# Gated loop and feed-forward block on one core: two queues for the first gate load, and a later place for three weight fetches

## The chip, the cores and the metric

The kernel runs on one core of a Trainium2 chip. A core has a matrix engine (TensorE, PE in the profile; its weight loads are PEld), a vector engine (VectorE, DVE), a scalar engine (ScalarE, ACT), a general engine (GpSimd, POOL) and a queue engine (SyncE, SP). Transfers between the device memory and the core's own memory are issued by SP, ACT or POOL and carried by 16 DMA engines. Each engine works through its own list of instructions in order. The metric is the time of one execution on the device, in microseconds (us); the median of 7 runs of the kernel before is 748.93 us, from 748.06 to 753.47.

## The reference, cut to what matters

The input has 4 batches, 8 heads, 768 time steps and 48 features. A complex gate `a` first gets its magnitude limited, then drives a recurrence over time; its output goes through a feed-forward block of width 2048.

```python
mag = np.sqrt(a_re * a_re + a_im * a_im)
scale = np.minimum(mag, 0.999) / (mag + 1e-06)
a_re_n, a_im_n = (a_re * scale, a_im * scale)
for t in range(S):
    new_re = ar * S_re - ai * S_im
    new_im = ar * S_im + ai * S_re
    S_re, S_im = (new_re + k_t v_t^T, new_im)
    y[:, :, t] = q_t . S_re
x = y.transpose(0, 2, 1, 3).reshape(B * S, H * D)     # 3072 x 384
h = x @ w_in                                          # 384 x 2048
out = np.maximum(h, 0.0) ** 2 @ w_out                 # 2048 x 384
```

## The kernel before, in words

**Units.** The work is cut into 8 units: 4 batches, each in two halves of 384 time steps. A unit's 8 heads make 4 pairs, and two pairs make a half z of the unit (z = 0 and 1). For each unit the kernel

- loads `a`, `q`, `k` (per half z, real and imaginary part of `a` apart) and `v` (in three chunks);
- normalises `a` in elementwise steps on ACT and DVE: `sq` and `sqi` square the two parts, `m2` adds them, `ln`, `ex` and `s2` make an inverse root, `r1` and `r2` are a Newton step, `n1`, `n2`, `l1`, `l2` scale `a`;
- multiplies the gates up over time (`in..`, `tot`, a tree of `scan` products, `bk`, `xn`), which gives the decay up to each step;
- multiplies `q` and `k` by these decays (`f`, `P`, `QK`). The result is called Q~ and K~ below; in the code it is the tile `QK`;
- writes K~ to device memory in time order (`rows`) and reads it back in another layout (`KC`), pair by pair for units 0 and 1;
- per pair: transposes (`tq`), scores (`sa`), masks (`A`), multiplies K~ and v (`kv`), adds up the state (`S`), mixes (`mix`), copies out (`y`) and places the result in `xT` by DMA;
- runs the feed-forward block: 16 blocks `h` (three matmuls each; for the first three blocks the first two matmuls are a step of their own, `h0`), `relu` and `g` on ACT, and the projection `o` in 3 chunks of 4 parts.

**Weights.** They arrive as 64-bit numbers and are turned into 32-bit ones on the chip: 16 pieces of `w_in` and 16 of `w_out`, each with a fetch (384 KB), a step `lower` on ACT and three steps `cv` on DVE. The first 13 pieces wait only for the first unit's `a` (`gate`, a small POOL copy that really reads `a`). Pieces 13 to 15 reuse the buffers of pieces 0 to 2. The `w_in` pieces are fetched by POOL, the `w_out` pieces by SP.

**What sets the order.** Every step is entered with an engine, a cost, a delay until its result can be used (`lag`), a rank and a list of steps that it depends on. `lay_out` (line 579) goes through the steps like a scheduler and gives each a start in its own model of time; the instructions are then emitted in that order, and `emit` ties each engine's instructions to that order. The dependencies in these lists are the planner's: in the program, an instruction waits only where it shares data with another (a tile that it reads, or a buffer that it reuses). `queue` is SP for units 0 and 1 and POOL after them (line 762). `fetch` is line 648, `weight_steps` line 694, the loads are `load` and `load_v` (lines 772 and 780), `square` is line 816, and `rows` (line 1186) holds both the write (line 1194) and the read back (line 1201).

**The profile's lines.** L777 is every load of `a`, `q` and `k`, L783 that of `v`, L667 a weight fetch, L825 and L828 the squares of the first unit, L832 the sum, L835 the ACT steps after it, L840 the Newton steps, L1194 and L1201 the rows of K~ and the reading back (KC), L1320 `kv`, L1360 the copy before `xT`, L1367 the DMA into `xT`, L1437 `h`, L1454 `o`. L1094 is a matmul without use of its result (`busy`, ten steps of two instructions in each of the units 0 and 1).

Of the kernel before, what the change touches and what calls it, by code (L numbers as in the profile page):

```python
# [481 lines left out]
def fast_path(ctx, tc, q, k, v, a_re, a_im, moe_w_in, moe_w_out, out, flag):  # L482
# [211 lines left out]
    def weight_steps():  # L694
        for i in range(2 * NF):
            if i < FIRST:
                deps = [("gate", z) for z in range(2)]
            elif i < NF:
                deps = [("cv", i - FIRST, 2)]
            elif i in LENT:  # L700
                deps = [("mix", 0, NP - 1), ("xT", 0, NP - 1, 1)]
            elif i < NF + NRAW:
                deps = [("cv", i - (NF - NF // 2), 2)]
            else:
                deps = [("cv", i - NRAW - (len(LENT) if i < NF + 2 * NRAW + len(LENT) else 0),
                         2)]
            step(("fetch", i), "SP" if i >= NF else "POOL", 600 if i >= NF else 750, 400 + i,
                 deps, lambda i=i: fetch(i), 7000)
            rank = CONV[i // NF] + i
            step(("lower", i), "ACT", 470, rank, [("fetch", i), ("e2", 0, 1)], lambda i=i: lower(i))  # L710
            for part, cost in enumerate((270, 470, 470)):
                step(("cv", i, part), "DVE", cost, CONV[i // NF] + i // 2 * 6 + part * 2 + i % 2,
                     [("cv", i, part - 1), ("lower", i) if part == 2 else ("fetch", i),
                      ("ap", 0, 1)],
                     lambda i=i, part=part: convert(i, part))
# [42 lines left out]
    def chain_steps(u):  # L758
# [10 lines left out]
        def src(ap):  # L769
            return ap[u["b"], :, ts(u["half"], L), :]  # L770

        def load(name, z, j):
            if j == 0:
                u[name, z] = nat.tile([C, 2, HH, W, D], F32, name=f"{name}{z}",
                                      tag=f"{name}{z}")
            ap = {"a": (a_re, a_im), "qk": (q, k)}[name][j]
            get.dma_start(out=u[name, z][:, j].rearrange("p h c d -> p h (c d)"),  # L777
                          in_=src(ap)[ts(z, HH)].rearrange(LOADS, c=W))

        def load_v(j):  # L780
            if j == 0:
# [4 lines left out]
        for name in ("a", "qk"):  # L786
            for z in range(2):
                for j in range(2):
                    add(("ld", n, name, z, j), queue, issue,
                        [("f", n - 1, z, i, r) + x for i in range(2) for r in range(2)  # L790
                         for x in ((), (0,), (1,))]
                        if name == "a" else [("ap", n - 1, z)]
                        + [("KC", n - 1, 1, i) for i in (NP // 2, NP - 1)]
                        + ([("xT", 0, NP - 1, h) for h in range(2)] if n == 1 else []),
                        lambda name=name, z=z, j=j: load(name, z, j),
                        lag=(3100 + 1100 * z + 300 * j if name == "a" else 8000)
                        if n == 0 else 6000)
        for j in range(W):
            add(("v", n, j), queue, issue,
                [("mix", n - 2, NP - 1), ("kv", n - 2, NP - 1), ("rest", n - 2, 2)]  # L800
                + ([("e2", 0, 1)] if n == 1 else []),
                lambda j=j: load_v(j), lag=27000 if n == 0 else 8000)
        if n == 0:

# [10 lines left out]

        def square(z, r=None):

            if not r:
                u["fa", z] = wk.tile([C, 2, HH, W, D], F32, name=f"fa{z}", tag=f"fa{z}")
                u["fb", z] = wk.tile([C, 2, HH, W, D], F32, name=f"fb{z}", tag=f"fb{z}")  # L820
            if r is None:
                act.activation(out=whole(u["fa", z]), in_=whole(u["a", z]), func=AF.Square,
                               accum_out=sums[:, n, z:z + 1])
            elif r == 0:
                act.activation(out=parts(z)[0], in_=flat(u["a", z][:, 0]), func=AF.Square)  # L825
            else:
                a = flat(u["a", z][:, 1])
                dve.tensor_tensor(out=parts(z)[1], in0=a, in1=a, op=ALU.mult)  # L828
# [71 lines left out]

        D1, A1 = dve_cost(NEL), act_cost(NEL)
        if n == 0:
            one("sq", "ACT", A1, lambda z: [("ld", n, "a", z, 0)], lambda z: square(z, 0))
            one("sqi", "DVE", D1, lambda z: [("ld", n, "a", z, 1), ("sq",)],
                lambda z: square(z, 1))
            one("ms", "ACT", A1 + 90, lambda z: [("m2",), ("me",)],
                lambda z: measure(z, parts(z)[2], AF.Copy), rank=900)
            add(("minus",), "ACT", 190, [("me", 0, 1)],
                lambda: act.mul(out=minus, in_=ident, mul=-1.0), rank=910)
        else:  # L910
            one("sq", "ACT", act_cost(2 * NEL) + 90,
                lambda z: [("ld", n, "a", z, 1), ("ap", n - 1, z), ("carry", n - 1, 0)],
                square)
# [295 lines left out]
        for z in range(2):  # L1209
            of_z = range(z * NP // 2, (z + 1) * NP // 2)  # L1210
            was_read = [("tq", n - 1, i, c) for i in of_z for c in range(W)] + [
                ("rows", n - 1, z, i) for i in of_z]
            add(("ov", n, z), "DVE", D1, [("xn", n, 2), ("rest", n, z), ("kk", n, z)],
                lambda z=z: over_k(z), rank=late(z))
            done = []
            for i, r in ((i, r) for i in range(2) for r in range(2)):
                for j in range(2):
                    if early or i == 0:
                        add(("f", n, z, j, j ^ r) + ((i,) if early else ()), "DVE",
                            dve_cost(NEL // 2 if early else NEL),  # L1220
                            [("xn", n, j)] + scans[-1],
                            lambda z=z, j=j, r=r, i=i if early else None:
                            cross(z, j, j ^ r, i))
                if not early:
                    continue
                P = ("P", n, z, r, i)
                qk = [("QK", n, z, j, r, i) for j in (1, 0)]
                add(P, "PE", 970, [("f", n, z, 0, r, i), ("f", n, z, 1, 1 - r, i), ("ov", n, z)]
                    + was_read + [("minus",)], lambda z=z, r=r, i=i: join_pe(z, r, i),
                    rank=-3000 if z == 0 else -1950 + 40 * n, bank="sc", until=qk[1])  # L1230
                for j, key in zip((1, 0), qk):
                    add(key, "DVE", 410, [P, qk[0] if j == 0 else P],
                        lambda z=z, j=j, r=r, i=i: apply(z, j, r, i))
                    done.append(key)
            for r in () if early else range(2):
                add(("join", n, z, r), "DVE", D1, [("f", n, z, 0, r), ("f", n, z, 1, 1 - r)],
                    lambda z=z, r=r: join(z, r))
            if not early:
                for j in (1, 0):
                    for r in range(2):  # L1240
                        add(("QK", n, z, j, r), "DVE", D1,
                            [("join", n, z, r), ("ov", n, z)] + was_read,
                            lambda z=z, j=j, r=r: apply(z, j, r))
                        done.append(("QK", n, z, j, r))
            add(("ap", n, z), "DVE", 0, done, lambda: None)
            for i in pairs_of(z):
                whole_z = not early
                keys = [x for x in done if x[3] == 1 and (whole_z or x[5] == i % 2)]
                pairs = of_z if whole_z else [i]
                for name, lag, deps in (  # L1250
                        ("rows", 4800 if whole_z else 3800,
                         keys + [("KC", n - 1, z, x) for x in of_z]),
                        ("KC", 7000 if whole_z else 4200,
                         [("rows", n, z, pairs[0])] + [("kv", n - 1, x) for x in of_z])):
                    add((name, n, z, pairs[0]), "POOL", 750, deps,
                        lambda z=z, i=pairs[0], name=name: rows(z, i, name == "KC"),
                        rank=-100, lag=lag)
                    for x in pairs[1:]:
                        add((name, n, z, x), "POOL", 0, [(name, n, z, pairs[0])],
                            lambda: None)  # L1260
# [331 lines left out]
```

## Time and profile before

| what | value |
|---|---|
| median of 7 runs | 748.93 us (748.06 to 753.47) |
| the profiled execution, its own time | 749.56 us |
| its span from the first to the last instruction | 747.8 us |
| mean granted TensorE clock | 0.997 |
| PE busy | 706.0 us, 94% |
| DVE busy | 509.0 us, 68% |
| ACT busy | 411.9 us, 55% |
| POOL busy | 115.0 us, 15% |
| read from and written to device memory | 56.62 MB, 14.16 MB |

The page gives busy time by engine, the span in 40 slices, the DMA queues, the chain of work that ended last and the costliest groups. The answers of the trace give instructions in order of time with the idle time before each in brackets and what ended it, the waits of an engine added up, busy times by stretch, and for each DMA the time from its issue to its landing. An issue in such a list is the time in which a queue (SPq, ACTq, POOL) hands a transfer over, not the transfer. Idle time of an engine matters only where it is the one that the others wait for.

### The profile page before, as it was taken

How to read it: one execution, taken by the hardware profiler on the slowest of the kernel's cores; microseconds unless marked ns; L12 is line 12 of the kernel's file. 1: busy time of each engine (PE TensorE's matmuls, PEld its weight loads, DVE VectorE, ACT ScalarE, POOL GpSimd, SP SyncE). 2: the span in 40 equal slices, each digit the busy share in tenths (PEclk: the TensorE clock that was granted, in tenths of full speed). 3: DMA queues.
4: the chain of work that ended last, by engine and by line, in shares of the span. 5: the costliest groups of instructions: out<-in, count | busy, mean ns of one | idle time of the engine just before them, and what ended most of it. 6: DMA issues, size and time to landing. Idle time of an engine off the chain costs nothing.

```text
span 747.8 us, 10017 instructions
## 1 busy us (share of the span) xinstructions
PE 706.0 (94%) x3578; PEld 474.7 (63%) x3578; DVE 509.0 (68%) x1204; ACT 411.9 (55%) x764; POOL 115.0 (15%) x165
## 2 busy tenths in 40 slices
PE   0389999999999999999999999999999999999996
PEld 0258556586667767766775677677667655555553
DVE  5999999978698898799469896988971564000000
ACT  6556594266938658853976479677365204402500
POOL 5013100052013013012210211130020431000000
PEclk9999999999999999999999999999999999999999
DMA  9617750054026115224510431261032684000000
GB/s 265 199 59 210 260 189 12 21 168 129 1 74 198 29 50 168 82 59 128 163 46 3 161 120 29 63 200 49 27 109 82 193 292 170 0 24 11 1 11 25
DMA packets 39196, 76.25 MB, mean 102 GB/s; under 512 B 10881, under 2 KB 25313, under 8 KB 39137
## 3 DMA queue, kind: packets, MB, share of 16 engines
q0 software_dynamic: 14336, 53.88, 23.0%
q1 hardware_dynamic: 24672, 21.49, 9.4%
q8 instruction: 30, 0.49, 0.3%
q14 instruction: 30, 0.24, 0.1%
q10 hardware_dynamic: 128, 0.15, 0.1%
HBM read 56.62 MB, written 14.16 MB: 95 GB/s over the span
## 4 chain that ended last, share of the span: by engine, by line
PE 90%; DMA 3%; SPq 2%; DVE 2%; ACT 0%; issue 0%; ACTq 0%
PE o L1454 33%; PE h L1437 32%; PE sa L1306 6%; PE tq L1293 5%; PE kv L1320 3%; PE P L1177 2%; PE ypair L1345 2%; SPq L783 2%; DMA v<-in_v_dram 1%; PE ypair L1350 1%; PE bk L979 1%; DMA xT<-yt 1%; PE tot L979 1%; PE y L1345 1%; PE busy L1094 1%; SPq L777 1%
## 5 line engine op out<-in xcount | busy, mean ns | idle before, releaser
L1437 PE MATMUL h<-xT,w 128*128 128x384 f32 x768 | 257.0, 487 | 1.6 <-DMA xT<-yt 1.6
L1454 PE MATMUL o<-w,g 128*128 128x384 f32 x768 | 255.7, 487 | 0.0
L1454 PEld LDWEIGHTS o<-w,g 128*128 128x128 f32 x768 | 142.9, 190 | 91.8 <-issue 0.4
L1437 PEld LDWEIGHTS h<-xT,w 128*128 128x128 f32 x768 | 142.2, 190 | 92.7 <-issue 2.8
L1444 ACT ACTIVATE g<-h 128x384 f32<-128x384 f32 x128 | 62.2, 487 | 82.0 <-PE h L1437 81.4
L1298 ACT COPY QKT<-tq 96x512 f32<-96x512 f32 x96 | 77.4, 872 | 33.9 <-PE tq L1293 33.7
L1459 ACT COPY ot<-o 128x384 f32<-128x384 f32 x24 | 11.5, 477 | 124.6 <-PE o L1454 124.6
L1447 ACT ACTIVATE g<-g 128x384 f32<-128x384 f32 x128 | 66.0, 523 | 2.9
L1293 PE MATMUL tq<-ident,QK 128*96 128x128 f32 x384 | 51.9, 273 | 1.4 <-DVE QK L1183 1.4
L1312 DVE TENSOR_TENSOR A<-sa,mask 128x384 f32<-128x384 f32 x64 | 35.2, 554 | 24.7 <-PE sa L1306 23.2
L1306 PEld LDWEIGHTS sa<-QKT 96*128 96x128 f32 x384 | 47.8, 192 | 6.1 <-issue 0.8
L1306 PE MATMUL sa<-QKT 96*128 96x128 f32 x384 | 51.4, 278 | 0.1
L1044 DVE TENSOR_TENSOR fa<-e 128x192 f32<-128x192 f32 (+4 forms) x144 | 48.1, 373 | 3.8 <-ACT e L1015 1.6
L1293 PEld LDWEIGHTS tq<-ident,QK 128*96 128x96 f32 x384 | 43.0, 126 | 11.9 <-issue 7.9
L979 PE MATMUL tot<-ident,last 128*128 128x128 f32 x72 | 12.3, 296 | 30.0 <-ACT last L886 24.4
L840 DVE SCALAR_TENSOR_TENSOR fb<-fb 128x576 f32<-128x576 f32 x48 | 34.9, 758 | 5.5 <-ACT fb L835 5.2
L832 DVE TENSOR_TENSOR fb<-fa 128x576 f32<-128x576 f32 x32 | 24.0, 755 | 20.0 <-ACT fa L945 15.3
L1051 DVE TENSOR_TENSOR e<-fa,fa 128x96 f32<-128x96 f32 (+6 forms) x160 | 35.5, 284 | 2.6
L835 ACT ACTIVATE fa<-fb 128x576 f32<-128x576 f32 x48 | 31.0, 676 | 10.7 <-DVE fb L832 6.1
L1194 POOL DMA_DIRECT2D rows<-QK x20 | 12.6, 631 | 156.3 <-DVE QK L1183 155.4
L783 POOL DMA_DIRECT2D v<-in_v_dram x18 | 15.9, 888 | 116.3 <-PE y L1350 78.0
L1183 DVE TENSOR_TENSOR QK<-qk,fa 128x576 f32<-128x576 f32 x48 | 33.2, 753 | 0.0
(125 smaller groups left out, 870.2 us busy)
## 6 DMA issues: line engine op xcount, KB each, us to landing
rows<-QK POOLq DMA_DIRECT2D x12, 576.0 KB, 3.9
raw<-in_moe_w_in_dram POOLq DMA_DIRECT2D x16, 384.0 KB, 7.5
look<-in_moe_w_in_dram POOLq DMA_DIRECT2D x16, 384.0 KB, 5.1
look<-in_moe_w_out_dram POOLq DMA_DIRECT2D x16, 384.0 KB, 4.3
raw<-in_moe_w_out_dram SPq DMA_DIRECT2D x13, 384.0 KB, 4.9
out_dram<-ot SPq DMA_DIRECT2D x24, 192.0 KB, 1.9
v<-in_v_dram POOLq DMA_DIRECT2D x18, 192.0 KB, 4.2
a<-in_a_re_dram POOLq DMA_DIRECT2D x12, 288.0 KB, 3.5
```

Source lines behind the costliest of these rows:

```text
L840: dve.scalar_tensor_tensor(out=f[dst[-1]], in0=f[2] if i == 0 else f[dst[0]], scalar=scalar, in1=f[by], op0=ALU.add if i else ALU.mult, op ...
L1044: dve.tensor_tensor(out=t, in0=x(e), in1=y(e)[:, j].unsqueeze(1) .to_broadcast(shape), op=ALU.mult)
L1051: dve.tensor_tensor(out=dst(u["e"])[:, r], in0=temp(0)[:, r], in1=temp(1)[:, 1 - r], op=ALU.add if r else ALU.subtract)
L1183: dve.tensor_tensor(out=outs(z)[j][:, hi, :, r * D:(r + 1) * D], in0=u["qk", z][:, j, hi], in1=p, op=ALU.mult)
L1293: nc.tensor.transpose(ps[:, 2 * j + h], src, ident)
L1298: act.copy(out=u["T", i].rearrange("r z (p c) -> r c z p", c=W)[:, c], in_=u["tq", i, c])
L1306: nc.tensor.matmul(sa[:, j], lhsT=T[:, 2 + h, ts(j, C)], rhs=T[:, h, ts(j, C)], start=True, stop=True)
L1312: dve.tensor_tensor(out=u["A", i][:, h], in0=u["sa", i, h], in1=mask3, op=ALU.mult)
L1437: nc.tensor.matmul(u["h", f], lhsT=w1[:, f, m], rhs=u["xT"][:, m], start=(m == 0), stop=(m == NM - 1))
L1444: act.activation(out=t, in_=u["h", f], func=AF.Relu)
L1447: act.activation(out=u["g", f], in_=u["g", f], func=AF.Square)
L1454: nc.tensor.matmul(u["o", c], lhsT=u["g", f][:, ts(c, C)], rhs=w2[:, f], start=(f == 0), stop=(f == NF - 1))
```

## The change

The diff does five things.

1. For the first unit, the imaginary parts of `a` are issued by ACT and the real parts by SP (before, SP issued all four).
2. In the planner's lists, the first unit's `q` and `k` loads depend on the second `sqi`, and its `v` loads on the last `k` load. `sqi` no longer depends on `sq`; the second half's `sq` depends on the first half's `ln`. `square` allocates its tiles in whichever of the two squares comes first.
3. Weight pieces 13 to 15 also depend on the write of the fourth pair's rows of K~ of unit 0.
4. The loads of `a` of the second half of unit 1 also depend on the read back of that pair (`KC`).
5. The planner's delays are other numbers: 3300 + 1300 z for the first `a` (before 3100 + 1100 z + 300 j), 4300 for `rows` of a pair (before 3800), 4600 for `KC` of a pair (before 4200).

```diff
@@ weight_steps
             elif i < NF:
-                deps = [("cv", i - FIRST, 2)]
+                deps = [("cv", i - FIRST, 2), ("rows", 0, 1, NP - 1)]
@@ chain_steps, load
-            get.dma_start(out=u[name, z][:, j].rearrange("p h c d -> p h (c d)"),
+            (nc.scalar if by_act(name, j) else get).dma_start(out=u[name, z][:, j].rearrange("p h c d -> p h (c d)"),
                           in_=src(ap)[ts(z, HH)].rearrange(LOADS, c=W))
+
+        def by_act(name, j):
+
+            return n == 0 and name == "a" and j == 1
@@ chain_steps, the loads' steps
-                    add(("ld", n, name, z, j), queue, issue,
+                    add(("ld", n, name, z, j), "ACT" if by_act(name, j) else queue, issue,
                         [("f", n - 1, z, i, r) + x for i in range(2) for r in range(2)
                          for x in ((), (0,), (1,))]
+                        + ([("KC", 0, 1, NP - 1)] if z and n == 1 else [])
                         if name == "a" else [("ap", n - 1, z)]
                         + [("KC", n - 1, 1, i) for i in (NP // 2, NP - 1)]
+                        + ([("sqi", 0, 1)] if n == 0 else [])
                         + ([("xT", 0, NP - 1, h) for h in range(2)] if n == 1 else []),
                         lambda name=name, z=z, j=j: load(name, z, j),
-                        lag=(3100 + 1100 * z + 300 * j if name == "a" else 8000)
+                        lag=(3300 + 1300 * z if name == "a" else 8000)
                         if n == 0 else 6000)
         for j in range(W):
             add(("v", n, j), queue, issue,
                 [("mix", n - 2, NP - 1), ("kv", n - 2, NP - 1), ("rest", n - 2, 2)]
-                + ([("e2", 0, 1)] if n == 1 else []),
+                + ([("e2", 0, 1)] if n == 1 else [("ld", 0, "qk", 1, 1)] if n == 0 else []),
                 lambda j=j: load_v(j), lag=27000 if n == 0 else 8000)
@@ square
-            if not r:
+            if ("fa", z) not in u:
@@ the first unit's squares
-            one("sq", "ACT", A1, lambda z: [("ld", n, "a", z, 0)], lambda z: square(z, 0))
-            one("sqi", "DVE", D1, lambda z: [("ld", n, "a", z, 1), ("sq",)],
-                lambda z: square(z, 1))
+            one("sq", "ACT", A1, lambda z: [("ld", n, "a", z, 0)] + z * [("ln", n, 0)],
+                lambda z: square(z, 0))
+            one("sqi", "DVE", D1, lambda z: [("ld", n, "a", z, 1)], lambda z: square(z, 1))
@@ rows and KC
-                        ("rows", 4800 if whole_z else 3800,
+                        ("rows", 4800 if whole_z else 4300,
                          keys + [("KC", n - 1, z, x) for x in of_z]),
-                        ("KC", 7000 if whole_z else 4200,
+                        ("KC", 7000 if whole_z else 4600,
```

## The prediction

> **What bounds the kernel now.** I read the page's busy lines first, then a table of stretches, then what TensorE (PE) waited for, then the order of time around the two places that the change touches.
>
> ```profile
> PE 706.0 (94%) x3578; PEld 474.7 (63%) x3578; DVE 509.0 (68%) x1204; ACT 411.9 (55%) x764; POOL 115.0 (15%) x165
> ```
>
> PE is busy for 706.0 of 747.8 us, and the page's slices put nearly all its idle time into the first two (digits 0 and 3). The stretches show what fills them:
>
> ```profile
> 20.00:40.00 20.00, 9.42 (x25) 5.42 (x26) 19.23 (x52) 13.72 (x28) 0.64 (x1) 1.00 0.58 164
> ...
> 60.00:80.00 20.00, 19.54 (x197) 16.59 (x197) 18.71 (x52) 11.25 (x18) 6.50 (x9) 1.00 0.61 177
> ```
>
> The columns after the stretch are its length, then PE, weight load, DVE, ACT and POOL busy, the clock, the DMA share and GB/s. From 20 us VectorE (DVE) is the full engine (19.23 of 20), and from 60 us PE is (19.54). What PE waited for between 40 and 90 us:
>
> ```profile
> PE bk L979 <- DVE e L1051: 1.9, 1, 1.9
> PE tq L1293 <- DVE QK L1183: 1.4, 1, 1.4
> PE h L1437 <- DMA xT<-yt: 1.3, 1, 1.3
> PE kv L1320 <- DMA KC<-rows: 0.4, 1, 0.4
> ```
>
> After 90 us the same view has one wait of 0.3 us up to 200 us and none from there to 748. So the end moves only by what moves the first PE work of unit 0, or by what opens or closes a PE gap before about 145 us. The front, in order of time:
>
> ```profile
> 0.81 1.28 ACT L525 ACT_TABLE_LOAD   x1 [0.81 <-PEq L1576]
> ...
> 2.39 0.51 SPq L777 DMA_DIRECT2D a<-in_a_im_dram  x1
> ...
> 7.53 18.42 SPq L783 DMA_DIRECT2D v<-in_v_dram  x6
> ...
> 8.43 0.76 DVE L828 TENSOR_TENSOR fa<-a 128x576 f32<-128x576 f32 x1 [1.68 <-DMA a<-in_a_im_dram]
> ...
> 10.14 0.67 ACT L835 ACTIVATE fa<-fb 128x576 f32<-128x576 f32 x1
> ...
> 12.27 0.76 DVE L840 SCALAR_TENSOR_TENSOR fb<-fb 128x576 f32<-128x576 f32 x1 [0.45 <-ACT fb L835]
> ```
>
> The last of a's four pieces (real and imaginary part of two halves) lands at 8.43 us, and 3.84 us later (square, sum, log, exponential, square) DVE starts the Newton step of the second half. From 12.27 us DVE is almost without gaps (11.5 of the 11.7 us to 24) until bk at 43.72, so a shift at 12.27 reaches PE. The chain that ended last names the v loads up to 30.88; DVE is busy on both sides of that moment, so I take it for a loosely attributed release. The other place:
>
> ```profile
> 69.14 0.76 POOL L1201 DMA_DIRECT2D KC<-rows  x1 [0.23 <-DMA rows<-QK]
> ...
> 75.22 1.22 PE L1320 MATMUL kv<-v,KC 128*96 128x48 f32 x12 [0.41 <-DMA KC<-rows]
> ...
> 83.03 1.21 PE L1437 MATMUL h<-xT,w 128*128 128x384 f32 x3 [1.30 <-DMA xT<-yt]
> ```
>
> POOL wrote the fourth pair's rows at 65.00 and two weight fetches at 67.41 and 68.16 before it came to that pair's read of K~ (KC), which takes 6.0 us to land; PE waits 0.41 us for it, works through mix and three partial h blocks (77.60, 4.14 us), and then waits 1.30 us for xT.
>
> **The change, part by part.**
>
> *q, k and v "behind the arrival" of a.* The new dependency (on the second imaginary square) is one of the planner's alone: there is no shared data, so it sets the order on a queue and makes nothing wait. The trace shows the kind: unit 1's v loads depend in the same way on a step of ACT that runs at 31.72, yet all six v issues begin between 7.53 and 20 us. SP (SyncE) has nothing else to do first, so q's first load, now behind two a issues and not four, goes out at about 1.84 instead of 2.94: 1.1 us earlier. Nobody needs it: k lands by 11.9 us and is first used at 31.59; v is first read at 39.52, and unit 0's last v lands by 24.4. Cost nothing, unless the earlier q slows a.
>
> *Imaginary parts of a issued by ACT.* Two issues (0.50 and 0.51 us on SP) move to ACT, whose two later issues took 0.53 and 0.60. The trace doesn't show whether ACT can issue while it loads its table (0.81 to 2.09). Early end: the second ACT issue begins at about 1.30, so 1.09 earlier, and the landing goes from 8.43 to 7.3; if also the 2.4 us hole between the second and third landing (5.12 to 7.55) closes to the 0.87 us of the landings after it, to 6.6. Late end: ACT issues after the table, second issue at 2.09 + 0.60 = 2.69, 0.30 late and beside q and k; at 0.87 us for each 288 KB piece that goes first, two pieces make 8.43 + 1.74 = 10.2. I take 8.0: the DMA share is 0.17 up to 2.5 us and 1.03 to 1.10 from there to 10, so only the ramp can be used, by about one issue length.
>
> [...]
>
> *Log of the first half ahead of the square of the second on ACT.* Log can go at 5.99 + 0.80 = 6.79 instead of 8.14. The second log needs real-part landing + 0.59 + 0.70 + 0.59, and imaginary-part landing + 1.71 (10.14 - 8.43). With unchanged landings (7.55 and 8.43) these give 9.43 and 10.14: no gain by itself, since the sum of the second half still sets it. With both parts landing at 8.0 (two queues share the engines, so the real part, 7.55 before, comes later): 9.88 against 10.14, front **-0.26 us**. Ends: with 6.6 for both, the log of the first half at 6.79 holds: 6.79 + 0.59 + 1.88 = 9.26, -0.88; with 10.2, +1.77.
>
> *The last three of the 16 first weights' pieces behind the fourth pair's rows.* Again planner order: on POOL, KC comes ahead of all three fetches. The rows write landed in 3.9 us with fetches beside it, 2.7 for the first two pairs; KC in 6.0, the second and third pair's in 3.6 and 3.7. So KC lands between 67.7 + 3.6 = 71.3 and 75.2. PE is at work until 74.81: gain 0.41, or 0 at the late end. DVE's 0.48 us wait for kv (76.47) goes too, which matters: at 144.5 PE's next bk and the DVE product that it reads are ready within 0.1 us of each other, so a gain on PE alone would be lost there. The pieces land about 2 us later (75 to 78); their conversion starts at 83.55, which covers 5 us. Late next: xT. From mix's end to xT's landing are 5.4 us, of which h hides 4.14; the 1.30 stays. **-0.41**.
>
> *Second half of unit 1's a behind KC.* These two SP issues (58.50, 58.91) come after xT of the third pair, near 75. The POOL rows write at 59.21 that ran beside them (4.8 us instead of 2.7) gets free, so KC of the third pair and the rows at 65.00 come up to 1 us earlier, inside the range above. Cover for a: its square (69.39) feeds a DVE sum at 101.27, 20 us later. Its price is a collision: 576 KB go out just ahead of xT of the fourth pair (78.27, landing in 4.68 and 4.4). At 0.87 us a piece that is 0 to +1.7 us on the 1.30 gap. Issued near 75 they should be down by 78: I take 0.
>
> *Lags (500 and 400 more), tile allocation in whichever square comes first:* no instructions; they only reorder. DVE and PE are in order, so a bad order costs its wait; the bounds are the four PE waits above, none to double.
>
> Sum: -0.26 - 0.41 = **-0.67 us**. The profiled execution took 749.56 (span 747.8); the median of the runs is 748.93, 0.63 under it. 749.56 - 0.67 - 0.63 = **748.3**.
>
> **The rivals.**
>
> *A. More is won.* Landing at 6.6 (-0.88), KC (-0.41), and xT's gap closed (-1.30) make -2.6: 746.3. For: the hole at 5.12 to 7.55 looks like an accident of some packets. Against: xT's gap has no mechanism here. Without it 747.6.
>
> *B. ACT's issue stands behind the table load.* +1.77 - 0.41 = +1.4: 750.3. For: the table row spans just that time. Against: POOL and SP rows show nothing that would tie an issue to the engine's work.
>
> *C. The other side: xT queues behind moved loads.* Place: SP's queue and the DMA engines at 75 to 83 us. Moved there are 576 KB of a and 3 x 384 KB of weights, 6 pieces of 288 KB; if all were outstanding at 78.27, 6 x 0.87 = 5.2 us, so PE's gap grows from 1.30 to 6.5: 748.93 - 0.67 + 5.2 = 753.5. It outweighs the gains from one piece on, and passes 0.3% from 3.4 pieces on (2.25 + 0.67 = 2.9 us). For: 4.68 us to land already, and 5.6 at 68.7 beside two fetches, where the xT at 73.7 to 75.1 took 2.1 to 3.1. Against: before, all three fetches landed by 76.7.
>
> *D. It doesn't do what it says and nothing moves:* 748.9.
>
> **How the numbers follow.** 0.3% (2.25 us) is about what a measurement of this kernel can tell from no change. Forecast (-0.67, with D beside it) 0.42, A 0.18, B 0.12, C 0.28. Faster by over 0.3% needs nearly all three terms of A: 0.14 of its 0.18. Slower by over 0.3% is C from 3.4 pieces on, or fewer with B's +1.77 beside them: 0.30. Within: the rest, 0.56. The likeliest case alone spans 747.4 (landing at 6.9) to 749.3 (KC gains nothing, landing 0.4 late). For 8 in 10 the range goes down to 746.5, which leaves about 0.08 of A below it, and up to 753.0, which leaves about 0.1 of C above.
>
> **What would show it.** Right: q's first issue near 1.84 and ahead of any arrival; ACT issues at 0.8 to 1.4; second Newton chain at 12.0; no PE wait for KC; h near 82.3. Wrong: ACT issues after 2.09; a PE wait for xT over 1.3 us; ACT or DVE waiting for fetched weights between 74 and 84; bk at 144 waiting for DVE.

## The result, and the profile after

The changed kernel takes 747.68 us (median of 19 runs, 746.88 to 748.91), the kernel before, timed beside it, 749.62 (47 runs, 748.06 to 753.47). The ratio is 0.9968, with a 95% interval from 0.9959 to 0.9978: 0.32% faster, about the 0.3% that the prediction took as the least that a measurement of this kernel can tell from no change. The profiled execution took 747.49 us (span 745.8) against 749.56 (747.8).

The direction and the range of the prediction hold; the forecast of 748.3 asks for 0.6 to 0.7 us of gain, and 1.9 came. The prediction had put 0.56 on a change of less than 0.3% either way and 0.14 on a gain of more; the interval covers both. In the changed kernel a line number past L825 is higher by six (h is L1443, o is L1460, KC is L1207).

The page's busy line and two stretches of the changed kernel (columns as before: length, PE, weight load, DVE, ACT and POOL busy, clock, DMA share, GB/s):

```profile
PE 704.3 (94%) x3578; PEld 473.4 (63%) x3578; DVE 505.9 (68%) x1204; ACT 411.8 (55%) x764; POOL 115.4 (15%) x165
```

```profile
20.00:40.00 20.00, 10.14 (x27) 5.82 (x28) 19.16 (x54) 14.45 (x29) 0.32 (x1) 1.00 0.52 153
60.00:80.00 20.00, 18.81 (x184) 15.64 (x183) 19.28 (x55) 11.02 (x18) 7.62 (x9) 1.00 0.60 166
```

No instruction was taken out, as forecast: the counts are the same. But from 60 to 80 us PE is busy for 0.73 us less than before and DVE for 0.57 more: DVE has become the fuller engine there. What PE waited for between 40 and 90 us:

```profile
PE bk L985 <- DVE e L1057: 1.7, 1, 1.7
PE tq L1299 <- DVE QK L1189: 1.7, 1, 1.7
PE ypair L1351 <- DVE A L1318: 1.2, 1, 1.2
PE h L1443 <- DMA xT<-yt: 1.1, 1, 1.1
PE P L1183 <- DVE fa L1170: 0.4, 1, 0.4
```

The wait for KC (0.4) is gone, and a wait for A of 1.2 that the kernel before didn't have stands in its place. The front in order of time:

```profile
0.81 1.28 ACT L525 ACT_TABLE_LOAD   x1 [0.81 <-PEq L1582]
0.81 0.99 SPq L777 DMA_DIRECT2D a<-in_a_re_dram  x2
0.84 1.06 ACTq L777 DMA_DIRECT2D a<-in_a_im_dram  x2
...
1.84 0.51 SPq L777 DMA_DIRECT2D qk<-in_q_dram  x1
...
7.61 0.76 DVE L834 TENSOR_TENSOR fa<-a 128x576 f32<-128x576 f32 x1 [0.65 <-DMA a<-in_a_im_dram]
...
11.57 0.76 DVE L846 SCALAR_TENSOR_TENSOR fb<-fb 128x576 f32<-128x576 f32 x1 [0.45 <-ACT fb L841]
```

ACT hands both pieces over between 0.84 and 1.90, while its own table load runs from 0.81 to 2.09. The last piece lands at 7.61 (8.43 before), and the Newton step of the second half starts at 11.57 (12.27). The other place, POOL's order and then PE's:

```profile
62.37 0.84 POOL L1200 DMA_DIRECT2D rows<-QK  x1 [3.87 <-DVE QK L1189]
63.19 0.78 POOL L1207 DMA_DIRECT2D KC<-rows  x1
65.52 1.04 POOL L1207 DMA_DIRECT2D KC<-rows  x1 [1.55 <-DVE w L692]
66.56 1.52 POOL L667 DMA_DIRECT2D raw<-in_moe_w_in_dram  x2
```

```profile
72.23 1.14 PE L1326 MATMUL kv<-v,KC 128*96 128x48 f32 x12
73.21 0.90 PE L1312 MATMUL sa<-QKT 96*128 96x128 f32 x6
...
75.64 0.53 PE L1351 MATMUL ypair<-A,v 128*48 128x128 f32 x5 [1.19 <-DVE A L1318]
...
82.14 2.17 PE L1443 MATMUL h<-xT,w 128*128 128x384 f32 x6 [1.13 <-DMA xT<-yt]
```

The fourth pair's KC goes out at 65.52 instead of 69.14, and kv now stands ahead of the pair's second score product (sa), so that this product's mask A reaches DVE late.

The gain in the two profiled executions: 0.72 us at bk (43.72 to 43.00), 1.44 at the first transpose (50.39 to 48.95), 0.89 at h behind xT (83.03 to 82.14), 0.90 at the first o (110.20 to 109.30), 1.56 at unit 1's first h (177.72 to 176.16), 2.0 at the end. Half of the 1.44 is no work of the change: before, PE ran at half clock (granted clock 0.50) from 44.19 to 47.60, and here it didn't (1.00 from 41 to 49 us). From bk to the first transpose before takes 6.67 us for it, against 5.95 here. Most of this stands in the later gains too: from bk to h before takes 39.31 us with a wait for KC of 0.41, and e4 below, with the same order on PE, a wait of 0.5 and no half clock, 38.69. So about 0.6 of the 0.89 at h, and by estimate as much behind it, is this one stretch in the profile of before.

### The profile page after: what moved, and what is told of

Its sections match the earlier page's. It is cut to its first block, busy times and chain, and to the rows that moved or that the text cites. A ratio compares the mean times of both kernels' runs of the same rounds, so it can differ in the third digit from the quotient of the medians.

```text
span 745.8 us, 10021 instructions
## 1 busy us (share of the span) xinstructions
PE 704.3 (94%) x3578; PEld 473.4 (63%) x3578; DVE 505.9 (68%) x1204; ACT 411.8 (55%) x764; POOL 115.4 (15%) x165
## 4 chain that ended last, share of the span: by engine, by line
PE 86%; DVE 8%; DMA 3%; SPq 2%; issue 1%; ACT 0%; ACTq 0%; DVEq 0%
PE h L1443 32%; PE o L1460 29%; PE tq L1299 6%; PE sa L1312 6%; PE kv L1326 3%; PE ypair L1351 2%; DMA v<-in_v_dram 2%; PE P L1183 2%; PE ypair L1356 2%; DVE fa L1050 1%; SPq L787 1%; DVE e L1057 1%; PE tot L985 1%; PE y L1351 1%; PE bk L985 1%; PE y L1356 1%
## 5 line engine op out<-in xcount | busy, mean ns | idle before, releaser
L1443 PE MATMUL h<-xT,w 128*128 128x384 f32 x768 | 256.7, 487 | 1.1 <-DMA xT<-yt 1.1
L1460 PE MATMUL o<-w,g 128*128 128x384 f32 x768 | 255.4, 487 | 0.0
L1460 PEld LDWEIGHTS o<-w,g 128*128 128x128 f32 x768 | 142.9, 190 | 91.8 <-issue 0.4
L1443 PEld LDWEIGHTS h<-xT,w 128*128 128x128 f32 x768 | 142.3, 190 | 91.9 <-issue 2.1
L1057 DVE TENSOR_TENSOR e<-fa,fa 128x96 f32<-128x96 f32 (+6 forms) x160 | 35.4, 284 | 2.6
```

The costliest lines, as they stand in the source:

```text
L1057: dve.tensor_tensor(out=dst(u["e"])[:, r], in0=temp(0)[:, r], in1=temp(1)[:, 1 - r], op=ALU.add if r else ALU.subtract)
L1443: nc.tensor.matmul(u["h", f], lhsT=w1[:, f, m], rhs=u["xT"][:, m], start=(m == 0), stop=(m == NM - 1))
L1460: nc.tensor.matmul(u["o", c], lhsT=u["g", f][:, ts(c, C)], rhs=w2[:, f], start=(f == 0), stop=(f == NF - 1))
```

## The experiments

Each kernel was timed beside the kernel before on the same chip. "Gate" is the start of POOL's second copy of a, which waits for the last landing only. "h" is the first h behind the last xT of unit 0, and "QK1" is DVE's first product QK of unit 1. All are from one profile each. "Calm" is the median span of the executions with a mean clock of at least 0.998, and "long" counts executions over 1.5 us above it (calm spans come from 45 executions of before, 13 of after, and 3 in e6 to 10 in e10). The kernels with a wait for KC are those that fetch weights ahead of it. The profiles of before, e8 and e11 have 3.4 us at half clock behind bk (0.50 in before and e8, worked out for e11), which holds their first transpose back by about 0.6 us (6.57 to 6.67 us behind bk, against 5.95 to 5.96 in the others), and h and the first o with it.

| kernel | time, us | ratio, 95% interval | gate | PE's wait for KC | h | first o | QK1 | calm | long |
|---|---|---|---|---|---|---|---|---|---|
| before | 749.62 to 750.69 | 1 | 8.46 | 0.4 | 83.03 | 110.20 | 148.48 | 747.0 | 44 of 106 |
| after | 747.68 | 0.9968, 0.9959 to 0.9978 | 7.63 | none | 82.14 | 109.30 | 145.59 | 745.5 | 1 of 21 |
| e1 ACT issues | 748.42 | 0.9990, 0.9974 to 1.0005 | 7.28 | 0.8 | 81.70 | 108.87 | 147.09 | 746.5 | 2 of 12 |
| e2 SP issues | 747.80 | 0.9971, 0.9959 to 0.9982 | 8.13 | none | 82.32 | 109.48 | 145.76 | 745.8 | 0 of 12 |
| e3 fetches later | 748.33 | 0.9980, 0.9966 to 0.9994 | 8.44 | none | 81.67 | 108.84 | 147.02 | 746.5 | 1 of 12 |
| e4 more filling | 749.85 | 0.9998, 0.9982 to 1.0015 | 7.99 | 0.5 | 81.86 | 109.02 | 147.27 | 747.7 | 3 of 12 |
| e5 fetches early | 749.46 | 0.9989, 0.9973 to 1.0005 | 7.37 | 0.3 | 81.86 | 109.03 | 146.20 | 746.6 | 4 of 12 |
| e6 lags alone | 750.13 | 1.0013, 0.9995 to 1.0032 | 7.03 | 1.1 | 82.55 | 109.72 | 147.72 | 747.9 | 5 of 12 |
| e7 nine steps | 748.98 | 0.9987, 0.9970 to 1.0004 | 7.99 | 1.4 | 82.70 | 109.86 | 148.16 | 746.7 | 4 of 12 |
| e8 no fillers in unit 1 | 747.61 | 0.9965, 0.9951 to 0.9980 | 7.46 | none | 82.58 | 109.74 | 145.69 | 745.7 | 0 of 12 |
| e9 two parts | 747.56 | 0.9977, 0.9967 to 0.9987 | 7.36 | none | 80.58 | 107.74 | 145.94 | 745.8 | 0 of 11 |
| e10 held by data | 747.47 | 0.9970, 0.9955 to 0.9986 | 6.63 | none | 81.48 | 108.64 | 145.60 | 745.7 | 0 of 11 |
| e11 KC lag 5800 | 748.77 | 0.9995, 0.9983 to 1.0006 | 7.13 | none | 82.04 | 109.21 | 145.18 | 746.9 | 0 of 11 |
| e12 parts, hold, eight steps | 746.93 | 0.9964, 0.9950 to 0.9978 | 6.65 | none | 80.42 | 107.59 | 145.79 | 745.1 | 0 of 5 |

### ACT's issue, alone and taken out

e1: the kernel before, with this line alone (the order of everything else as before):

```diff
-            get.dma_start(out=u[name, z][:, j]...
+            (nc.scalar if n == 0 and name == "a" and j == 1 else get).dma_start(out=u[name, z][:, j]...
```

> The kernel before with its order untouched; only the imaginary parts of the first unit's a are issued by ACT. Landing theory: the last part lands near 7.6 us instead of 8.43, bk starts near 43.0 instead of 43.72, and the time falls by 0.7 us (ratio 0.999). Order theory (the whole gain comes from the planner's new order): the landing may move, but the time stays within 0.2 us.

e2: the changed kernel, in which the planner still counts ACT as the issuer, but SP issues all four pieces:

```diff
-            (nc.scalar if by_act(name, j) else get).dma_start(out=u[name, z][:, j]...
+            get.dma_start(out=u[name, z][:, j]...
```

> The changed kernel's order, but SP issues all four parts of the first a. Landing theory: the last part lands near 8.4 us again, the second Newton chain starts at 12.3 instead of 11.57, and 0.7 us of the gain is lost (ratio to before 0.998). Order theory: the gain stays whole (0.9968).

The gate copies of e1 and of e2:

```profile
7.28 0.78 POOL L808 COPY gate<-a 128x1 f32<-128x1 f32 x1 [1.49 <-DMA a<-in_a_im_dram]
```

```profile
8.13 0.78 POOL L814 COPY gate<-a 128x1 f32<-128x1 f32 x1 [2.56 <-DMA a<-in_a_im_dram]
```

The issue by ACT brings the landing forward, but one profile doesn't say by how much: the six kernels with four issues on SP have gates from 7.03 to 8.46 (mean 8.01: before, e2, e3, e4, e6, e7), the six with two on ACT and no hold from 7.13 to 7.63 (mean 7.37: after, e1, e5, e8, e9, e11). So 0.64 us on average, and a spread of 1.4 us for the same issues by SP. Up to the tree it goes through: bk follows the gate by 35.1 to 35.4 us in all twelve. At the end it is worth 0.1 to 0.3 us in the changed kernel's order (e2 against after, by medians and by calm spans; the intervals overlap) and, in the order of before, 0.1% with an interval that holds zero (e1). So the landing alone doesn't carry the gain: e2 has nearly all of it with a landing half a microsecond later.

### The fetches, alone and taken out

e3: the kernel before with the one dependency:

```diff
-                deps = [("cv", i - FIRST, 2)]
+                deps = [("cv", i - FIRST, 2), ("rows", 0, 1, NP - 1)]
```

> The kernel before with only the new dependency of weight pieces 13 to 15. The prediction's reading: POOL issues KC of the fourth pair ahead of the three fetches, it lands by 73 us, PE's 0.41 us wait for KC goes and the time falls by 0.4 us. Rival: the order that the planner makes of it (the place of A and of the idle filler matmuls) moves more than that, either way by 0.5 to 1.5 us.

e5: the changed kernel with the same line turned back. Only POOL's order differs from the changed kernel.

> The changed kernel with one part undone: the last three pieces of the first weights are again free to be fetched before the rows of the fourth pair; TensorE's, SP's and the other engines' written orders stay those of the changed kernel, only POOL issues the third and fourth K~ between the fetches again. Theory K (the wait for KC is worth its length, 0.4 to 0.8 us, because TensorE is the bound from 82 us on): 747.7 + 0.4 = 748.1, a wait of kv for KC of 0.4 to 0.8 us shows and the wait for A of 1.2 us becomes shorter by as much or stays. Theory O (the gain lies in the written order, and A's lateness hides the KC wait): 747.5 to 747.9, no difference from the changed kernel, the A wait stays near 1.2. Theory C (it is idle stretches of TensorE between 50 and 82 us that call up the half clock in some executions): the executions spread up to 750 again, mean clock of 0.994 to 0.995 in some.

e3 is 0.2% faster than before, and its interval excludes zero: by itself this is the larger half of the change. PE's order is that of before; DVE and ACT take the weight steps in another order, as the planner made it, so e3 is not the one dependency alone. e5 is the cleaner pair with the changed kernel: without the dependency it loses most of its gain (0.9989 instead of 0.9968, though the intervals overlap a little). Theory K's wait of 0.3 us in e5's profile doesn't explain that: the A wait shrinks there by half a microsecond (0.7), and the profiled span is only 0.8 longer. DVE waits there for two pieces of w_out, 1.51 us against 0.35 in the changed kernel, and QK1 comes 0.61 later. What differs more is the executions that weren't profiled. By the column "long", kernels in which PE waits for KC have 62 long executions of 166, and those without the wait 2 of 95; the pairs before and e3 (44 of 106 against 1 of 12) and e5 and after (4 of 12 against 1 of 21) differ by the dependency. That is the spread that theory C forecast. It doesn't show the cause: the kernels with the wait are the ones with the fetches ahead of KC, so the count can't tell the wait from anything else that these fetches disturb. A lower clock goes with the length: of the 44 long executions of before, 42 have a mean clock of 0.996 or less, and of its 50 executions at 0.997 or more only 2 are long.

### Half clock: is it the gap ahead of bk?

e4: the kernel before, with three steps of filler doubled ahead of bk in unit 0 (extra matmuls without use), order untouched:

```diff
-                    [("scan", n, 3 + j // 2, "plus", 1), ("busy", n, j - 1)], busy,
+                    [("scan", n, 3 + j // 2, "plus", 1), ("busy", n, j - 1)],
+                    lambda more=2 if n == 0 and 6 <= j <= 8 else 1: busy(more),
```

> The kernel before with three more filler matmuls on PE ahead of bk of unit 0 (1.95 us of PE work in the gap from 41.85 to 43.72 us), order untouched. Clock theory: the half-speed stretch of 3.4 us that the profile of before shows from 44.19 us follows from that gap; it goes, tq starts 0.7 us earlier relative to bk, and the time falls by about 0.7 us. Rival: the stretch has nothing to do with the gap; it stays in the same share of executions, and the time rises by 0 to 0.2 us because the fillers end a little behind bk's operands.

It closes the gap (no wait before bk) and nothing is won: 0.9998, with 3 of 12 executions long. So nothing speaks for the half clock at 44 us in the profile of before as what makes its executions long. Two profiles speak against it. e8 and e11 have 3.4 us at half clock at the same place (43.18 to 46.57 and 42.69 to 46.10, worked out from mean clocks of 0.90 and 0.84 from 40 to 44 us and of 0.68 and 0.74 from 44 to 48, with the 0.50 that e8 shows at 43.5 to 43.7), and neither has a long execution. The rows of e8:

```profile
42.87 1.32 PE L985 MATMUL bk<-ident,e 128*128 128x128 f32 x6 [1.95 <-DVE e L1057]
...
49.45 1.05 PE L1299 MATMUL tq<-ident,QK 128*96 128x128 f32 x8 [1.43 <-DVE QK L1189]
```

That is 6.58 us from bk to the transpose instead of 5.95, and a span of 745.9 beside a calm one of 745.7. e6's profile caught another place. Two stretches of e6, lengths and columns as above:

```profile
72.00:75.40 3.40, 2.37 (x22) 1.99 (x24) 2.95 (x9) 0.80 (x2) 0.00 (x0) 1.00 0.24 66
75.40:78.80 3.40, 3.40 (x20) 2.66 (x21) 3.40 (x9) 0.48 (x1) 0.99 (x2) 0.50 0.00 0
```

with these waits of PE ahead of it:

```profile
72.73 1.22 PE L1320 MATMUL kv<-v,KC 128*96 128x48 f32 x12 [1.10 <-DMA KC<-rows]
...
75.34 0.84 PE L1345 MATMUL ypair<-A,v 128*48 128x128 f32 x5 [0.30 <-DVE A L1312]
...
77.60 4.73 PE L1437 MATMUL h<-xT,w 128*128 128x384 f32 x12
```

The clock is 0.50 for 3.4 us, from 2.7 us after the wait for KC ends, and the twelve h matmuls take 4.73 us instead of 4.14. The 3.4 us ahead of it hold 0.73 us of the wait for KC and the 0.30 for A. That this wait for KC was so paid for a second time is my estimate from these rows; no run shows that the one brings the other. Whether the long executions of before have the half clock at the same place is not shown: no trace of a long one was taken, e6's own profiled execution is not a long one (747.9, as its calm span), and why the A wait of the changed kernel, as long as e6's KC wait, goes with hardly any long execution stays open.

The four stretches (44.19 to 47.60, 75.4 to 78.8, and those of e8 and e11) have the same length of 3.4 us. PE was not idle throughout a time of that length ahead of them: it was busy for 1.53 us of it in before and for 2.37 us in e6, at a clock of 1.00. Nor does its busy share alone decide: e7's PE was busy for 1.20 of the 3.4 us from 39.9, and its clock stayed at 1.00. What calls up the half clock is not shown.

### The lags, alone

e6: the kernel before with the two lags (4300 and 4600).

> The kernel before with the two lags of rows and KC alone (3800 to 4300, 4200 to 4600). My prediction put this part at nothing: 749.9 (as the kernel before on the same chip), waits for KC and xT as before. Theory O (the planner's new order is most of the gain, and the lags are what turns it): 748.2 or less, rows of the fourth pair issued ahead of the third K~, the wait of unit 1 for xT gone and a filler step of unit 1 in the tail after the last o, as in the changed kernel.

Theory O falls in its strong form: no gain (1.0013, and the interval holds 1), and no filler step in the tail. But it isn't nothing either: the lags alone put kv of the fourth pair ahead of the second sa, as in the changed kernel. With the old lags, PE's order up to 190 us is that of before in e1, e3 and e9.

### Filler steps of unit 1

e7: `range(BUSY - n)` instead of `range(BUSY)` in the kernel before; e8: `range(BUSY if n == 0 else 0)` in the changed one.

> The kernel before with nine filler steps instead of ten in unit 1 (one busy step of two matmuls left out, which computes nothing that the output needs; the rest of the order nearly as it was). This prices a filler step that stands in TensorE's busy stretch. Theory O: 0.65 us less by the start to start distances (two matmuls of 0.33), so 749.3 against 749.9. If a filler step only fills an idle stretch it is worth nothing: 749.9.

> The changed kernel without any filler step in unit 1 (it leaves out 20 matmuls whose result nothing reads). In its trace 18 of them stand between 142.2 and 176.2 us, and TensorE idles there for 0.18 us only, so if each were in the way as theory O has it: 9 x 0.65 = 5.9 us less, 741.8. The rival: they stand where the chain through DVE and POOL would leave TensorE waiting anyhow, so that most of it turns into waits for QK, A and xT, and the clock may drop behind the idle stretches: 746 to 749. I expect 745.5.

In e7, the way from the first o to unit 1's first h is 66.96 us (67.52 before), 0.56 less, of which the wait for xT behind it takes 0.18 back; the ratio doesn't tell 0.4 us from zero. In e8 some of PE's other steps changed places too. I was wrong there by far: not 5.9 and not 2 us, but 0.1. What PE waited for in e8 after 90 us:

```profile
PE ypair L1351 <- DVE A L1318: 1.5, 2, 1.1
PE P L1183 <- DVE fa L1170: 1.1, 1, 1.1
PE h L1443 <- DMA xT<-yt: 0.8, 1, 0.8
PE P L1183 <- DVE QK L1189: 0.5, 1, 0.5
PE sa L1312 <- DVE QK L1189: 0.3, 1, 0.3
```

These are 4.2 us of waits in place of 5.9 us of fillers, 3.4 of them for DVE. In the changed kernel's order, PE isn't the bound in unit 1, though its busy time says 39.82 of 40 us: the fillers made it look so. QK1 shows the same: 145.59 to 146.20 in after, e2, e5, e8 and e10, which have this order, and not in the sequence of their first o (108.64 in e10 gives 145.60, 109.74 in e8 gives 145.69).

### Only the two parts

e9: the kernel before with the lines of e1 and e3 together, nothing else.

> The kernel before with two parts of the change alone: ACT issues a's imaginary halves of the first unit, and the last three pieces of the first weights wait for the rows of the fourth pair; the lags, the hold of the next unit's a and all the rest of the order stay as before. Theory P (these two parts are the change, the rest is at best nothing, as the lags alone showed): a ratio of 0.9965 to 0.9975, as the changed kernel's 0.9968, no wait for KC, and no execution under a mean clock of 0.9955. Theory O (the rest of the new order, with a filler step in the tail and no wait for xT in unit 1, carries about 1 us): a ratio of 0.998 to 0.9985, as with the fetches alone, the wait for xT in unit 1 still 0.3 to 0.8.

e9's order of time on PE:

```profile
80.58 3.79 PE L1437 MATMUL h<-xT,w 128*128 128x384 f32 x11 [0.78 <-DMA xT<-yt]
...
107.74 15.64 PE L1454 MATMUL o<-w,g 128*128 128x384 f32 x48
...
175.18 4.14 PE L1437 MATMUL h<-xT,w 128*128 128x384 f32 x12
180.06 3.14 PE L1437 MATMUL h<-xT,w 128*128 128x384 f32 x9 [0.75 <-DMA xT<-yt]
```

747.56, a calm span of 745.8, no long execution: the two parts are the change, as far as the time can tell. The ratio of 0.9977 lies between theory P's 0.9965 to 0.9975 and theory O's 0.998 to 0.9985, and its interval covers both. The rest moves the gain about. Up to the first o, e9 is 1.56 us ahead of the changed kernel, since it has no wait for A; in unit 1 it waits 0.75 for xT and has all its fillers on the way, while the changed kernel has lost its wait for xT there and does one filler step (two matmuls, 0.65 us) at 739.8, behind its last o. So theory P fits the sum, within what the interval can tell, and theory O was right that something else carries part of the gain in the changed kernel.

### q, k and v truly behind a's arrival

e10: the changed kernel with

```diff
             ap = {"a": (a_re, a_im), "qk": (q, k)}[name][j]
+            if n == 0 and name == "qk" and z == 0 and j == 0:
+                dve.tensor_copy(out=u["qk", 0][:, 0, 0, 0, 0:1], in_=u["a", 1][:, 1, 0, 0, 0:1])
```

> The changed kernel with q, k and v truly behind a's arrival: VectorE copies one element of the last a into the tile of q before q's first load, so that SP's queue stops there. My rival A put the last landing at 6.6 in that case and priced it at 0.88 us against 8.43. Expected: last a at 6.5 to 7.0 instead of 7.6, the second Newton chain at 10.5 to 10.9 instead of 11.57, the scan's bk 0.7 to 1.0 earlier. If that gain goes through to the end: 746.8. If q and k then come late or the gain is caught by VectorE's work between 45 and 80 us, as the issue by ACT was within this order (0.1 us for 0.5 us of landing): 747.5 to 747.8. I expect 747.5.

```profile
6.63 0.77 POOL L816 COPY gate<-a 128x1 f32<-128x1 f32 x1 [0.95 <-DMA a<-in_a_im_dram]
```

The landing is at 6.6, as rival A had it. bk comes at 42.54 (43.00 in the changed kernel), h 0.66 earlier, and unit 1's first h at 176.17 (176.16). The whole gain is gone by QK1, where DVE sets the time. DVE's own waits show where it went:

```profile
92.16 0.36 DVE L685 TENSOR_SCALAR w<-raw 128x384 uint32<-128x384 uint32 x1 [0.82 <-DMA raw<-in_moe_w_out_dram]
...
97.59 0.36 DVE L685 TENSOR_SCALAR w<-raw 128x384 uint32<-128x384 uint32 x1 [0.39 <-DMA raw<-in_moe_w_out_dram]
```

These 1.21 us for two pieces of w_out stand against 0.35 us for one piece in the changed kernel (97.15), and the DMA share from 80 to 84 us is 1.05 here and 1.04 there, where it is 1.01 from 84 to 100. So part of what DVE had won it spent waiting for w_out. 747.47, no difference from the changed kernel.

### Another lag of KC, and a version from all this

e11: the changed kernel with 5800 for 4600.

> The changed kernel with the lag of KC at 5800 instead of 4600, so that the planner puts kv of the fourth pair behind the second sa of that pair on TensorE, and A ahead of the sums of S on VectorE. In the changed kernel's trace ypair waits 1.19 us for that A, of which the three sums take 0.85. Theory A (this wait is on the path): it falls to 0.3 to 0.5, h starts 0.4 to 0.8 earlier, 747.1. Theory D (VectorE, busy without a break from 64 to 77 us, sets the end of the fourth pair in any order): the wait becomes one for S or for xT of the same length, 747.7.

The A wait is gone, and h comes at 82.04 instead of 82.14: theory D, though e11's profile has the half clock behind bk (about 0.6 us) and an earlier landing, which nearly cancel. From bk to h it takes 39.55 us, against 39.14 in the changed kernel. Less the 0.6, that is an estimated 0.2 us won of the 1.19. Waits of 0.5 for QKT and 1.0 for xT stand there, and DVE seems to set the end of the fourth pair. The calm span is 1.4 us longer than that of the changed kernel; unit 1 is ordered anew and waits 0.9 for xT.

e12: e9 with the hold of e10 (and the planner's two dependencies for q, k and v), and `range(BUSY - 2 * n)`.

> The version that the runs so far point to: the order of the kernel before, in which the earlier starts of the first unit went through to unit 1 (67.4 to 67.5 us from o to h in six kernels of that order, whatever came ahead), with the two parts that paid (ACT's issue, fetches behind the rows), with q, k and v held by data behind a's arrival, and with eight filler steps instead of ten in unit 1 (it leaves out four matmuls whose result nothing reads). Against the two parts alone (747.56): the hold 0.3 to 0.7 us at o, as in the changed kernel, now passed on; the two steps 0.4 to 1.0 at unit 1's h by the run with nine. Theory P (TensorE sets unit 1 in this order): 746.2 to 746.8, h of unit 1 at 173.6 to 174.2. Theory D (VectorE's chain sets unit 1 in this order too once TensorE is ahead): waits for A or QK appear behind 140 us and the time stays at 747.2 to 747.6.

```profile
107.59 15.64 PE L1457 MATMUL o<-w,g 128*128 128x384 f32 x48
...
174.44 4.14 PE L1440 MATMUL h<-xT,w 128*128 128x384 f32 x12
179.08 4.11 PE L1440 MATMUL h<-xT,w 128*128 128x384 f32 x12 [0.49 <-DMA xT<-yt]
```

746.93 us (5 runs, 746.46 to 747.58), a ratio of 0.9964 (0.9950 to 0.9978): faster than before, and by its calm span 0.4 us ahead of the changed kernel, though the intervals of the two overlap. The hold brought 0.15 us at o, not 0.3 to 0.7, and the two steps 0.6 at h. Unit 1's h, at 174.44, is a little later than theory P's 173.6 to 174.2. A wait of 0.3 for A behind 140 us shows that DVE is reached here too, as theory D had it.

## Why the prediction was right or wrong

**ACT's issue (-0.26).** Mechanism right, size wrong. The issue isn't held by the table load (0.84 to 1.90 beside 0.81 to 2.09), so rival B falls; q goes out at 1.84, as forecast, and waits for nothing. I took 8.0 for the landing by "about one issue length" off a single profile at 8.43; on average the landing goes from 8.01 to 7.37, and in the two profiles bk moved by 0.72. What I had not seen is that the landing of before scatters from 7.03 to 8.46 with the same issues. The 0.64 is less than the 1.09 by which the prediction's early end took ACT's second issue to come earlier. That the real part comes later with two queues is shown for the first half alone: its square starts at 4.99 instead of 3.89, but the second half's real part, issued at 1.30, lands 5.4 us later, at about 6.7 instead of 7.5.

**KC (-0.41).** The wait went, and its 0.48 on DVE with it, but the term is mis-sized. 0.41 is one draw: the six profiles of kernels with a fetch ahead of KC show 0.3, 0.4, 0.5, 0.8, 1.1 and 1.4. And it left out what the fetches ahead of KC do in the executions that weren't profiled. e3 measures the whole: 748.33 against 749.94 on the same chip, 1.6 us (0.4 to 2.5 by the interval), of which only 0.5 is in the calm span (747.0 to 746.5). This is the step that failed: a wait of a TensorE-bound kernel was priced at its length in one profile. That the rest is half clock behind the wait is my guess from the mean clocks (0.996 or less in 42 of the 44 long executions), not shown. The late pieces also kept ACT waiting: the prediction looked at their step on DVE (83.55), while `lower` on ACT waited 0.99 us for one, up to 73.56.

**The offset of 0.63.** I took the median to lie 0.63 under the profiled execution, as the first seven runs had it. The 47 runs beside the changed kernel have a median of 749.62, 0.06 above the profiled 749.56: the offset was a small sample of a wide spread (the 748.06 to 753.47 was on view). Without it the forecast would have been 748.9; so it hid half of the miss, and that the forecast came within 0.6 us of the measured time is luck to that extent.

**Lags and order (0).** The sum of this is near nothing (e9 against after), the step behind it failed: "the bounds are the four PE waits above, none to double" overlooked that a new order can open a fifth. It did (A, 1.19 us), for the lags turned kv and sa round. It was made good in unit 1: no wait for xT (0.34 before), and a filler step moved behind the last o (0.65). That h came at 82.14, near the 82.3 named as a sign, is luck in part: 0.72 at bk, 0.41 for KC and about 0.6 of half clock in the profile of before went, and the wait of 1.19 came.

**The second half of a of unit 1 (0), and rival C.** The two issues went out at 69.03 and 69.60, not near 75, 8 us ahead of the xT that ACT issued at 77.53. The wait for xT went from 1.30 to 1.13; the collision that C needs didn't come. This part wasn't tried alone on the chip.

**Rival A** had its landing in e10 and e12 (6.6) but not its gain; waits for xT of 0.7 and 1.3 us stayed there. **Rival D** falls: the interval excludes 1. **The pair at 144.5** (PE's bk and DVE's product ready within 0.1 us of each other) was the right place to look. In the order of before, QK1 follows the first o by 38.2 to 38.3 us in before, e1, e3, e4, e9 and e12: PE sets it, and gains go through. In the new order DVE sets it at 145.6 to 146.2, in e5 and e10 after waits for w_out, and they don't.

The gain by executions, then: 747.0 to 745.5 in calm spans, 1.5 us, and 748.25 to 745.9 over all spans, 2.35. The second figure sets four chips of before against one of the changed kernel; timed beside each other the two differ by 1.94. So the long executions that the change removed are worth about 0.4 to 0.85 us of the median.

## What to carry to other kernels

A wait of the bounding engine for a transfer is priced from several profiles or kernels, not from one, and where the times of before spread upward, the granted clock of each execution tells whether lost clock goes with it (here 0.996 or less in 42 of 44 long ones). Two profiled executions differ by such a stretch too (3.4 us at 0.50, about 0.6 us here): take it out before crediting a gain. Before crediting a gain at the front, find the next place where another engine sets the time, and don't trust an engine's full busy share there if part of it is filling: take the fillers out and see what it waits for. Look at that next place for transfers as well as for work. Planner delays are no cost-free part of a change; the written order that they make is to be compared first.

## What was not expected of the hardware

- ACT issued two transfers from 0.84 to 1.90 us while its table load ran from 0.81 to 2.09.
- The last of four pieces of 288 KB landed between 7.03 and 8.46 us in six kernels with the same issues on SP, between 7.13 and 7.63 with two of them on ACT, and at 6.6 with nothing issued behind them.
- TensorE's clock fell to 0.50 for 3.4 us behind a stretch of 3.4 us in which it was busy for 2.37 us (e6). Behind the gap ahead of bk it fell in the profiles of before, e8 and e11 and not in those of the changed kernel, e2, e3, e5, e7 and e10, with waits of 1.7 to 2.2 us in all.
